# Second MoE's input weights in a fused attention and MoE kernel: a scale for each pair of combined items, made while the pieces are narrowed

## The chip, the core and the metric

The kernel runs on one core of a Trainium2 chip. The metric is the device time of one execution in microseconds (us). Three runs of the kernel before gave 968.54 to 969.66 us.

## What is computed

```python
attn = softmax(rotate(q) @ rotate(k).T / sqrt(64)) @ v      # 4 batches x 8 heads x 576 rows x 64
x  = attn.reshape(2304, 512)
h  = maximum(x @ w1, x @ w2, x @ w3);  x = h @ w_out        # first MoE:  512 -> 768 -> 512
h  = x @ w_in;  g = h * sigmoid(h);  out = g @ w_out        # second MoE: 512 -> 2048 -> 512
```

The weights arrive as 64-bit floats, everything else as 32-bit. The second MoE's `w_in` has 512 x 2048 numbers, its `w_out` 2048 x 512.

## The kernel before

**Attention** runs over 80 tiles of 128 (or 64) query rows. For each tile TensorE (PE) makes the scores (lines 440, 443, 433, 434), VectorE (DVE) takes the row maximum (`nb`, line 453), ScalarE (ACT) the exponential (460) and the normalisation (472). Four DMAs on SyncE's queue move the result into the turned layout (`pt`, 511), DVE turns its 32 x 32 blocks (533), and PE multiplies by `v` (574, 578). The scores have one PSUM tile, so the next tile's scores wait until ACT has read this one's.

**Filler.** Between the tiles PE gets the first MoE's matmuls (line 673), in groups, by a budget per tile; DVE and ACT take the groups' results out of PSUM (690, 692, 698, 699). What is not done when the last tile has its scores runs after attention, and then the second MoE starts (lines 1071, 1103, 1166). All matmuls of both MoEs split their operands into a high and a low half float, each scaled by a power of two.

**The second MoE's weights** are prepared beside attention, one step per tile and two in every fourth tile, from tile 21 on (`wprep3`, the loop at line 1331). `narrow_w2` (820) first handles `w_in` (`WI`), then `w_out` (`WO`), each in 32 pieces of 128 x 256: SyncE loads a piece as 64-bit numbers (858), ACT and DVE narrow it to 32 bits (229; 241, 248, 249), ACT measures its largest square (155), and SyncE writes it to a scratch in memory (833 for `WI`, 838 for `WO`). When all 32 pieces of `WI` are measured, `scale_a` and `scale_b` make one scale for the matrix: three small DVE operations take the root (`root`, 160 to 162), one the row maximum (263), PE transposes it (122), DVE reduces it (124), PE spreads it by a product with ones (130), and four small DVE operations make the powers of two (145 to 148).

From then on `prep_w8` (954, `wprep4`) reads the scratch back in 16 items of 128 x 512 (965), each four blocks. GpSimd (POOL) makes four sums of blocks (971). ACT casts the eight blocks to the high half (`cast_high`, 948) and DVE makes the low half (`cast_low`, 952), in two casts of 128 x 512 each, and SyncE writes each half item to another scratch, `w8scr` (979), from which the second MoE loads them. `WO`'s scratch is read by `prep_w7` (989) after attention.

**What sets the order.** Each engine runs its instructions in the order of its program; a scheduler makes that order from the order of emission and from `issue_after`, which holds an instruction behind another one (`cast_low` and the narrowing on DVE behind the newest row maximum, `cast_high` behind the newest exponential, the scale's PE steps behind the newest scores). Rings of buffers bound how far the steps run apart: 4 pieces (`z_p`), 2 items (`za_p`), 2 sums (`zs_p`), 3 cast halves (`w8o`).

Of the kernel before, what the change touches and what calls it, by code (L numbers as in the profile page):

```python
# [22 lines left out]
def fused_kernel(  # L23
# [796 lines left out]
    def narrow_w2(W, src, nm):  # L820
# [3 lines left out]
        part = {}  # L824
        M = W.m * 512 // 256
        for n in range(M + 5):
            if n >= 5:
                W.measure(n - 5)
# [10 lines left out]
            if 3 <= n <= M + 2:  # L839
                with tc.issue_after(last["max"]):  # L840
                    W.narrow_low(part.get(n - 3))
                    W.narrow_b(n - 3, part.pop(n - 3, None))
            if 2 <= n <= M + 1:
                if wide:
                    W.t[n - 2] = z_p.tile([P, 256], F32, tag="z", name="z")
                with tc.issue_after(exps[-1]):
                    W.narrow_a(n - 2, part.get(n - 2), low=False)
            if n < M:
                i, o = divmod(n * 256, 512)
                if nm == "wi":  # L850
                    q, c = divmod(i, KC)
                    from_ = src[c * P:(c + 1) * P, q * 512 + o:q * 512 + o + 256]
                else:
                    from_ = src[i * P:(i + 1) * P, o:o + 256]
                if wide:
                    part[n] = z64_p.tile([P, 256], w1.dtype, tag="z64", name="z64")
                    with tc.issue_after(last["load"]):
                        nc.sync.dma_start(out=part[n], in_=from_)
                else:
                    W.t[n] = z_p.tile([P, 256], F32, tag="z", name="z")  # L860
                    nc.sync.dma_start(out=W.t[n], in_=from_)
            yield
        t = W.scale_a(n=M)
        yield
        with tc.issue_after(last["score"]):
            W.scale_b("s" + nm, t)
        yield
# [85 lines left out]

    def prep_w8(step):

        sw = half_of(WI, "wi")
        steps = []

        def item(k):
            f, c = divmod(k, 2)  # L960
            z, w = {}, {}

# [483 lines left out]
```

## Time and profile before

| | |
|---|---|
| three runs, us | 968.85, 968.54, 969.66 |
| the profiled execution, us | 970.68 |
| its span, first to last instruction, us | 969.0 |
| busy, share of the span: PE, DVE, ACT, POOL | 93%, 73%, 63%, 46% |
| granted TensorE clock, mean | 0.983 |
| DMA moved | 146.29 MB |

The profiled execution's time is its span and 1.7 us around it. Busy shares are averages over stages with different limits; the stages are told apart by time. A matmul's end is modelled, so PE's busy time says where PE had nothing at all, not that it ran at its best.

### The profile page before, as it was taken

The numbers are of one execution on the slowest core, as the hardware profiler recorded it, in microseconds if no ns is written. First come the engines' busy times: TensorE is split into PE (matmuls) and PEld (weight loads), VectorE is DVE, ScalarE is ACT, GpSimd is POOL, SyncE is SP. The second block draws the span as 40 slices with busy tenths as digits, with TensorE's granted clock in tenths as the row PEclk, the third lists the DMA queues.
The fourth block names the chain that finished last, engine by engine and source line by source line (L and its number), as shares of the span: only waits on it lengthen the run. The fifth ranks groups of instructions, "written<-read, shape, count | busy, mean of one in ns | idle before, by whom it ended". The sixth has DMA issues, their size and how long they took to land.

```text
span 969.0 us, 19018 instructions
## 1 busy us (share of the span) xinstructions
PE 901.6 (93%) x6802; PEld 669.0 (69%) x6802; DVE 709.6 (73%) x1271; ACT 609.4 (63%) x1405; POOL 441.1 (46%) x482
## 2 busy tenths in 40 slices
PE   3887998999999999989998999999998999999997
PEld 1443665666665666656654687788887888888886
DVE  6779888877788676898887677465786766856654
ACT  1987677757788777789877534363654545545442
POOL 6745485870325502321211047264486467464363
PEclk9799998999999999999999999999999999999999
DMA  6953035858888985899999763273543434424101
GB/s 154 285 146 108 14 100 126 186 110 179 200 172 196 221 159 135 218 241 228 263 223 204 183 206 110 63 230 113 157 158 99 136 122 136 127 87 137 61 1 44
DMA packets 178798, 146.29 MB, mean 151 GB/s; under 512 B 50960, under 2 KB 160272, under 8 KB 178704
## 3 DMA queue, kind: packets, MB, share of 16 engines
q1 hardware_dynamic: 177200, 144.36, 58.0%
q8 instruction: 54, 0.88, 0.4%
q10 hardware_dynamic: 1504, 0.72, 0.3%
q14 instruction: 40, 0.33, 0.1%
HBM read 90.51 MB, written 26.21 MB: 120 GB/s over the span
## 4 chain that ended last, share of the span: by engine, by line
PE 54%; DMA 8%; DVE 8%; ACT 5%; POOL 4%; issue 3%; SPq 3%; DVEq 0%; ACTq 0%; POOLq 0%
PE m L673 12%; PE m L1103 7%; DMA pt<-e 5%; PE mb L1103 5%; PE c L1166 4%; PE b L1166 4%; PE a L1166 3%; PE xp L578 3%; PE s L443 3%; PE mg L673 3%; POOL gsum L1050 2%; PE d L1166 2%; SPq L511 2%; DVE pt L533 1%; DVE nb L453 1%
## 5 line engine op out<-in xcount | busy, mean ns | idle before, releaser
L673 PEld LDWEIGHTS <-w 128*128 128x128 f16 x1632 | 159.1, 98 | 61.0 <-issue 17.8
L673 PE MATMUL m<-x,w 128*128 128x256 f16 (+1 forms) x1356 | 186.9, 286 | 10.6 <-DVE t L692 5.4
L1166 PEld LDWEIGHTS <-g 128*128 128x128 f16 x1485 | 145.8, 98 | 17.2
L1103 PEld LDWEIGHTS <-w8s 128*128 128x128 f16 x1344 | 131.2, 98 | 16.3 <-issue 1.0
L453 DVE TENSOR_REDUCE nb<-s 128x2 f32<-128x1152 f32 (+1 forms) x80 | 98.6, 1233 | 40.7 <-PE s L443 34.1
L460 ACT ACTIVATE e<-s,nb 128x576 f32<-128x576 f32 x144 | 105.3, 736 | 29.8 <-DVE nb L453 27.2
L472 ACT ACTIVATE e<-e,rec 128x576 f32<-128x576 f32 x144 | 104.1, 767 | 9.3 <-DVE rec L470 8.9
L366 POOL TENSOR_TENSOR w<-qk,sin_sb 128x512 f32<-128x512 f32 (+2 forms) x40 | 43.4, 1087 | 128.1 <-DMA qk<-in_q_dram 122.5
L443 PE MATMUL s<-T 64*128 64x512 f32 x256 | 80.7, 701 | 0.0
L578 PE MATMUL xp<-pt,vd 128*64 128x256 f32 (+1 forms) x512 | 76.5, 414 | 0.2 <-DVE pt L533 0.2
L533 DVE STREAM_TRANSPOSE pt<-pt 128x1024 f32<-128x1024 f32 (+1 forms) x60 | 67.7, 1129 | 11.9 <-DMA pt<-e 11.6
L971 POOL TENSOR_TENSOR zs<-za 128x128 f32<-128x128 f32 x32 | 17.1, 554 | 119.9 <-DVE w8o L952 46.1
L1117 POOL TENSOR_TENSOR z<-t 128x256 f32<-128x256 f32 x32 | 27.1, 847 | 89.0 <-DVE t L1109 53.9
L1055 DVE SCALAR_TENSOR_TENSOR g<-gsum,sg,g 128x1024 f16<-128x1024 f32 x36 | 49.2, 1372 | 24.5 <-ACT g L1054 24.1
L1054 ACT ACTIVATE g<-gsum,sg 128x1024 f16<-128x1024 f32 x36 | 40.9, 1143 | 37.8 <-POOL gsum L1050 37.8
L673 PE MATMUL m<-h,wo 128*128 128x256 f16 (+1 forms) x448 | 61.7, 286 | 0.0
L673 PEld LDWEIGHTS <-wo 128*128 128x128 f16 x512 | 49.7, 98 | 14.7 <-issue 2.0
L578 PEld LDWEIGHTS xp<-pt,vd 128*64 128x64 f32 x512 | 35.1, 136 | 34.4 <-issue 12.3
L944 POOL TENSOR_TENSOR z<-z 128x256 f32<-128x256 f32 x32 | 30.1, 964 | 42.1 <-DMA z<-zwo 41.6
L1166 PE MATMUL b<-w,g 128*128 128x256 f16 x376 | 48.5, 273 | 0.0
L1166 PE MATMUL c<-w,g 128*128 128x256 f16 x376 | 48.1, 274 | 0.0
L1166 PE MATMUL a<-w,g 128*128 128x256 f16 x376 | 47.9, 273 | 0.0
(266 smaller groups left out, 1998.1 us busy)
## 6 DMA issues: line engine op xcount, KB each, us to landing
w8s<-w8scr SPq DMA_DIRECT2D x64, 448.0 KB, 4.3
pt<-e SPq DMA_DIRECT2D x192, 128.0 KB, 4.1
z<-in_moe_w_in_dram SPq DMA_DIRECT2D x32, 256.0 KB, 3.6
z<-in_moe_w_out_dram SPq DMA_DIRECT2D x32, 256.0 KB, 3.9
w8scr<-w8o SPq DMA_DIRECT2D x32, 256.0 KB, 3.6
w<-in_moe_w_dram SPq DMA_DIRECT2D x6, 768.0 KB, 5.0
wo<-in_moe_w_dram SPq DMA_DIRECT2D x6, 768.0 KB, 5.4
qk<-in_q_dram SPq DMA_DIRECT2D x32, 128.0 KB, 3.6
```

The lines of the kernel that those rows point to most:

```text
L366: tt(out=w4, in0=t4, in1=sin2, op=ALU.mult)
L443: last["s"] = last["score"] = nc.tensor.matmul(s[:, o:o + 512], qs[r], kt[r], start=True, stop=True).ins
L453: x = nc.vector.tensor_reduce(out=nb[:, 0:m], in_=both(s, 0, 960, 576) if m > 1 else s[:, 0:576], op=ALU.max, axis=AX.X, negate=True)
L460: x = nc.scalar.activation(out=e[:, HK[g]], in_=s[:, SK[g]], func=AF.Exp, bias=nb[:, g:g + 1], accum_out=sm[:, g:g + 1])
L472: nc.scalar.activation(out=e[:, HK[g]], in_=e[:, HK[g]], func=AF.Copy, scale=r[:, g:g + 1])
L533: nc.vector.transpose(out=x, in_=x)
L578: nc.tensor.matmul(xp[r, 0:n], v4[:, g, c, :], turned(c, g), start=False, stop=(c == 3))
L673: x = nc.tensor.matmul(ps[:, 0:n], l, r, start=(first and i == 0), stop=(not more and i == len(passes) - 1))
L1054: nc.scalar.activation(out=h, in_=x, func=AF.Copy, scale=sg_t[jb])
L1055: nc.vector.scalar_tensor_tensor(out=l, in0=x, scalar=sg_t[jb], in1=h, op0=ALU.mult, op1=ALU.subtract)
L1103: nc.tensor.matmul(o, l, r, start=(i == 0), stop=(i == len(passes) - 1))
L1166: x = nc.tensor.matmul(ps, l, r, start=first, stop=last_, skip_group_check=True)
```

## The change

`w_in`'s pieces are loaded in another order and cut: two successive pieces now hold the four blocks of one item, and four successive pieces the two items of a pair. A piece is narrowed straight into its half of the item's tile (`za`, now a ring of four, and `z_p` is gone). As soon as the four pieces of pair f are measured, the pair gets a scale of its own (`scale_m`, `scale_a`, `scale_b`, one step each, `wi_scale`), eight in all. Then the sums and casts of its two items follow in the steps of `narrow_w2` itself, one high and one low cast per step. The scratch `zwi`, its 32 writes and its 16 reads are gone, and so is `prep_w8`. `WO` follows `WI` without a pause, and its scratch is written in 16 writes of two pieces. The one scale of the whole matrix is still made, from the maxima that are there, for the second MoE's activations. Since the second MoE's results now differ in scale from pair to pair, `ch` has eight columns, and the Silu of its first block of 256 rows (`s1`) runs on each 256-column half with its own column: 16 instructions of 128 x 256 where 8 of 128 x 512 stood.

```diff
@@ pools, scratch @@
-    z_p = right("z_p", 4)
...
-    zscr = {nm: dram.tile([P, KC * (F2 // 512) * 512], F32, name="z" + nm) for nm in ("wi", "wo")}
+    zscr = {nm: dram.tile([P, KC * (F2 // 512) * 512], F32, name="z" + nm) for nm in ("wo",)}
@@ narrow_w2 @@
-    def narrow_w2(W, src, nm):
...
-                if nm == "wi":
-                    i, o = divmod(n - 5, 2)
-                    q, c = divmod(i, KC)
-                    half, f = divmod(4 * q + 2 * o, HB)
-                    nc.sync.dma_start(
-                        out=zscr[nm].rearrange("p (f c a i n) -> p f c a i n", c=2, a=2, i=2, n=P)[:, f:f + 2, c % 2, c // 2, half],
-                        in_=W.t[n - 5].rearrange("p (f n) -> p f n", n=P),
-                    )
-                else:
-                    nc.sync.dma_start(out=zscr[nm][:, (n - 5) * 256:(n - 4) * 256], in_=W.t[n - 5])
...
+    half_wi = const.tile([P, HB], F32, name="half_wi")
+    inv_wi = const.tile([P, HB], F32, name="inv_wi")
+
+    def wi_scale(f, m):
+        e = rare.tile([P, 1], F32, tag="wie", name="wie")
+        ei, hi, ii = e.bitcast(I32), half_wi.bitcast(I32)[:, f:f + 1], inv_wi.bitcast(I32)[:, f:f + 1]
+        nc.vector.tensor_scalar(out=e, in0=m, scalar1=2.0 ** -45, scalar2=None, op0=ALU.max)
+        nc.vector.tensor_scalar(out=ei, in0=ei, scalar1=EXPMASK, scalar2=None, op0=ALU.bitwise_and)
+        nc.vector.tensor_scalar(out=hi, in0=ei, scalar1=-1, scalar2=266 << 23, op0=ALU.mult, op1=ALU.add)
+        nc.vector.tensor_scalar(out=ii, in0=ei, scalar1=13 << 23, scalar2=None, op0=ALU.subtract)
+
+    def narrow_w2(WI, WO):
+        part, z, zs, w, ma = {}, {}, {}, {}, {}
+        M = WI.m * 512 // 256
+        which = lambda n: (WI, n) if n < M else (WO, n - M)
+
+        def place(n):
+            W, i = which(n)
+            if n % 2 == 0:
+                z[n // 2] = za_p.tile([P, 4, P], F32, tag="za", name="za")
+            W.t[i] = flat(z[n // 2][:, n % 2 * 2:n % 2 * 2 + 2])
...
+                from_ = wi2[(2 * a + c) * P:(2 * a + c + 1) * P, :].rearrange("p (i f n) -> p f i n", i=2, n=P)[:, f]
...
+        def scale_m(f):
+            m = ma[f] = rare.tile([P, 1], F32, tag="wim", name="wim")
+            nc.vector.tensor_reduce(out=m, in_=WI.maxima(4 * f, 4), op=ALU.max, axis=AX.X)
+
+        def scale_a(f):
+            with tc.issue_after(last["score"]):
+                ma[f] = all_max_a(ma[f])
+
+        def scale_b(f):
+            with tc.issue_after(last["score"]):
+                m = all_max_b(ma.pop(f))
+            wi_scale(f, m)
...
+        for n in range(2 * M + 6):
+            for f in range(HB):
+                if 7 <= n - 4 * f <= 9:
+                    (scale_m, scale_a, scale_b)[n - 4 * f - 7](f)
...
+                for at_, g, q, h in ((10, low, k, 0), (11, low, k + 1, 0), (12, low, k, 1), (13, low, k + 1, 1)):
+                    if s == at_:
+                        g(q, h)
...
+                for at_, g, q, h in ((9, high, k, 0), (10, high, k + 1, 0), (11, high, k, 1), (12, high, k + 1, 1)):
...
+                if s in (8, 9):
+                    sums(k + s - 8)
...
+            if n >= M + 4 and n % 2 and n <= 2 * M + 3:
+                i = n - 4 - M
+                nc.sync.dma_start(out=zscr["wo"][:, (i - 1) * 256:(i + 1) * 256], in_=flat(z.pop((n - 4) // 2)))
@@ y_scales @@
-        ch = small.tile([P, 1], F32, tag="ch", name="ch")
-        nc.vector.tensor_scalar(out=ch, in0=co, scalar1=2.0 * w, scalar2=None, op0=ALU.mult)
+        ch = small.tile([P, HB], F32, tag="ch", name="ch")
+        nc.vector.tensor_scalar(out=ch, in0=inv_wi, scalar1=i, scalar2=2.0 * w, op0=ALU.mult, op1=ALU.mult)
@@ prep_w8, removed whole @@
-    def prep_w8(step):
...
-                nc.sync.dma_start(out=flat(z[0]), in_=zscr["wi"][:, (2 * f + c) * 512:(2 * f + c + 1) * 512])
...
-            for d, fn in ((0, load), (2, sums), (2.1, lambda: high(0)), (2.9, lambda: low(0)), (3, lambda: high(4)), (3.9, lambda: low(4))):
@@ s1 @@
-                nc.scalar.activation(
-                    out=g[:, 2 * half:2 * half + 2].rearrange("p t (i n) -> p i t n", i=2),
-                    in_=ps.rearrange("p (i t n) -> p i t n", i=2, t=2), func=AF.Silu, scale=ch,
-                )
+                for e in range(2):
+                    nc.scalar.activation(
+                        out=g[:, 2 * half:2 * half + 2, e * P:e * P + P],
+                        in_=ps[:, e * 256:e * 256 + 256].rearrange("p (t n) -> p t n", t=2), func=AF.Silu, scale=ch[:, 2 * u + e:2 * u + e + 1],
+                    )
@@ main loop @@
-    wprep3, wprep4 = narrow_all(), None
+    wprep3 = narrow_w2(WI, WO)
...
+            za_p.bufs = 4
             for _ in range(1 + (j % 4 == 0) if j > 20 else 0):
                 next(wprep3, None)
-            if hasattr(WI, "s"):
-                wprep4 = wprep4 or prep_w8(1.7)
-                next(wprep4, None)
```

**The order, first place.** DVE, from the row maximum of the 38th tile to that of the 39th, before (line numbers of each kernel's own file; `z` are pieces, `t`, `h` the first MoE's results):

```order
L453 TENSOR_REDUCE nb_3027<-s_3023 128x2
L533 STREAM_TRANSPOSE pt_2846<-pt_2846 128x1024
L241 TENSOR_SCALAR z_2_2872<-z_2_2872 128x256
L248 TENSOR_SCALAR z_2971<-z_2971 128x256
L692 SCALAR_TENSOR_TENSOR t_3156<-m_3143,t_3141 128x256
L249 SCALAR_TENSOR_TENSOR z_2971<-z_2_2872,z_2971 128x256
L692 SCALAR_TENSOR_TENSOR t_3171<-m_3158,t_3156 128x256
L470 RECIPROCAL rec_3102<-rec_3102 128x2
L699 TENSOR_TENSOR h_6_3173<-t_3171,h_6_3173 128x256
L453 TENSOR_REDUCE nb_3095<-s_3091 128x2
```

The same place now (`w8o` is a cast, `amax` a step of a pair's scale):

```order
L449 TENSOR_REDUCE nb_3142<-s_3138 128x2
L529 STREAM_TRANSPOSE pt_2939<-pt_2939 128x1024
L1020 SCALAR_TENSOR_TENSOR w8o_3077<-zs_2891,half_wi_141,w8o_3077 128x512
L240 TENSOR_SCALAR z_2_2968<-z_2_2968 128x256
L247 TENSOR_SCALAR za_3084<-za_3084 128x256
L123 TENSOR_REDUCE amax_3070<-tr_3068 1x1
L688 SCALAR_TENSOR_TENSOR t_3288<-m_3275,t_3273 128x256
L248 SCALAR_TENSOR_TENSOR za_3084<-z_2_2968,za_3084 128x256
L466 RECIPROCAL rec_3231<-rec_3231 128x2
L688 SCALAR_TENSOR_TENSOR t_3303<-m_3290,t_3288 128x256
L449 TENSOR_REDUCE nb_3224<-s_3220 128x2
```

One cast and one scale step have come in; one tile earlier 23 instructions now stand between two row maxima, three casts among them, where 10 stood. Counted over the order, the 32 low casts stand between the 29th and the 55th row maximum now, and behind the 55th before; between these two, 32 pieces are narrowed where 25 were.

**Second place.** DVE between the 64th and the 65th row maximum, before:

```order
L453 TENSOR_REDUCE nb_5182<-s_5178 128x2
L533 STREAM_TRANSPOSE pt_4985<-pt_4985 128x1024
L241 TENSOR_SCALAR z_3_4936<-z_3_4936 128x256
L248 TENSOR_SCALAR z_5130<-z_5130 128x256
L952 SCALAR_TENSOR_TENSOR w8o_5141<-za_4940,wihalf_4184,w8o_5141 128x512
L249 SCALAR_TENSOR_TENSOR z_5130<-z_3_4936,z_5130 128x256
L241 TENSOR_SCALAR z_0_5012<-z_0_5012 128x256
L248 TENSOR_SCALAR z_5220<-z_5220 128x256
L249 SCALAR_TENSOR_TENSOR z_5220<-z_0_5012,z_5220 128x256
L692 SCALAR_TENSOR_TENSOR t_5418<-m_5405,t_5343 128x256
L470 RECIPROCAL rec_5266<-rec_5266 128x2
L453 TENSOR_REDUCE nb_5259<-s_5255 128x2
```

and now:

```order
L449 TENSOR_REDUCE nb_5434<-s_5430 128x2
L529 STREAM_TRANSPOSE pt_5254<-pt_5254 128x1024
L240 TENSOR_SCALAR z_2_5218<-z_2_5218 128x256
L247 TENSOR_SCALAR za_5391<-za_5391 128x256
L578 SCALAR_TENSOR_TENSOR x_3917<-xp_5441,vs_3555,x_3917 128x320
L688 SCALAR_TENSOR_TENSOR t_5638<-m_5625,t_5577 128x256
L248 SCALAR_TENSOR_TENSOR za_5391<-z_2_5218,za_5391 128x256
L240 TENSOR_SCALAR z_3_5280<-z_3_5280 128x256
L247 TENSOR_SCALAR za_5391<-za_5391 128x256
L466 RECIPROCAL rec_5510<-rec_5510 128x2
L688 SCALAR_TENSOR_TENSOR t_5653<-m_5640,t_5638 128x256
L248 SCALAR_TENSOR_TENSOR za_5391<-z_3_5280,za_5391 128x256
```

The cast is gone from here, as from all tiles behind the 55th row maximum.

**Third place.** SyncE's queue around the 39th tile, before (`zwi` is the scratch of `w_in`, `pt` attention's moves):

```order
L858 DMA z_2_3404<-in_moe_w_in_dram 128x256
L833 DMA zwi_137<-z_3244 128x2x128
L308 DMA qk_3941<-in_k_dram 64x2x64
L511 DMA pt_3377<-e_3302 32x8x128 x4
L315 DMA vd_0_129<-in_v_dram 128x2x256
L320 DMA vd_0_129<-in_v_dram 64x64
L858 DMA z_3_3505<-in_moe_w_in_dram 128x256
L833 DMA zwi_137<-z_3342 128x2x128
```

and now:

```order
L304 DMA qk_3943<-in_k_dram 64x2x64
L860 DMA z_3_3375<-in_moe_w_in_dram 128x2x128
L507 DMA pt_3236<-e_3226 32x8x128 x4
L316 DMA vd_0_126<-in_v_dram 64x64
L876 DMA w8scr_133<-w8o_3190 128x2x512
L876 DMA w8scr_133<-w8o_3252 128x2x512
L316 DMA vd_0_126<-in_v_dram 64x64
L876 DMA w8scr_133<-w8o_3370 128x2x512
L507 DMA pt_3236<-e_3313 32x4x128
```

The scratch's writes are gone, and the writes of cast halves (`w8scr`) stand among attention's moves instead. Over the whole program SyncE has 395 rows where it had 456, DVE 1,330 where it had 1,262. The first MoE's matmuls move too: 424,448 of their columns stood behind the last tile's scores, and 412,288 do now; of the 12,160 that moved forward, 8,000 stand ahead of the 55th tile's scores and 4,160 behind them.

## Rows read from the trace of the kernel before

**Rows 1.** stretches: span, busy us (instructions) of PE, PEld, DVE, ACT, POOL; clock, DMA share, GB/s

```profile
218.00:378.00 160.00, 155.71 (x1052) 100.56 (x1052) 121.58 (x239) 121.00 (x344) 41.25 (x44) 1.00 0.84 179
378.00:537.00 159.00, 147.53 (x981) 93.30 (x978) 134.34 (x265) 131.97 (x364) 38.27 (x65) 1.00 0.92 226
537.00:624.00 87.00, 84.56 (x670) 64.37 (x669) 53.79 (x101) 37.01 (x70) 30.12 (x32) 1.00 0.47 132
...
760.00:969.00 209.00, 203.51 (x1863) 182.00 (x1860) 133.58 (x223) 96.70 (x147) 106.65 (x119) 0.99 0.31 94
```

**Rows 2.** who waited for whom on DVE, 218 to 378: us in total, times, longest

```profile
DVE nb L453 <- PE s L443: 15.1, 14, 2.9
...
DVE nb L453 <- PE s L434: 4.8, 4, 2.3
```

**Rows 3.** three shorter stretches, same columns as Rows 1

```profile
340.00:377.00 37.00, 37.00 (x244) 23.75 (x241) 24.69 (x52) 25.92 (x68) 0.00 (x0) 1.00 0.73 130
400.00:420.00 20.00, 18.99 (x133) 12.42 (x132) 19.55 (x37) 16.55 (x46) 3.75 (x8) 1.00 0.90 238
400.00:500.00 100.00, 94.08 (x650) 61.75 (x649) 88.60 (x176) 86.53 (x242) 18.03 (x36) 1.00 0.95 241
```

**Rows 4.** casts (tile w8o) alone, 378 to 537: DVE, ACT; clock, DMA share, GB/s

```profile
378.00:537.00 159.00, 23.46 (x29) 21.01 (x30) 1.00 0.92 226
```

**Rows 5.** two stretches, narrowed pieces (tile z) alone: DVE, ACT, POOL

```profile
218.00:378.00 160.00, 29.68 (x76) 23.56 (x77) 0.00 (x0) 1.00 0.84 179
378.00:537.00 159.00, 32.77 (x93) 28.01 (x91) 0.00 (x0) 1.00 0.92 226
```

**Rows 6.** DVE in order of time, 553 to 554.4: start, us, instruction

```profile
553.89 0.14 DVE L147 TENSOR_SCALAR swos<-swoe 128x1 int32<-128x1 int32 x1
553.95 0.14 DVE L148 TENSOR_SCALAR swoi<-swoe 128x1 int32<-128x1 int32 x1
554.07 0.15 DVE L939 TENSOR_SCALAR wohalf<-swos 128x1 f32<-128x1 f32 x1
```

**Rows 7.** DVE groups, 218 to 378: busy us, mean ns | idle before

```profile
L241 DVE TENSOR_SCALAR z<-z 128x256 uint16<-128x256 uint16 x25 | 14.1, 564 | 0.0
...
L249 DVE SCALAR_TENSOR_TENSOR z<-z,z 128x256 int32<-128x256 int32 x26 | 12.4, 477 | 0.2
```

**Rows 8.** DVE groups, 232 to 262

```profile
L241 DVE TENSOR_SCALAR z<-z 128x256 uint16<-128x256 uint16 x6 | 2.6, 427 | 0.0
L249 DVE SCALAR_TENSOR_TENSOR z<-z,z 128x256 int32<-128x256 int32 x6 | 2.5, 419 | 0.1
```

**Rows 9.** two more stretches, same columns as Rows 1

```profile
232.00:262.00 30.00, 30.00 (x206) 19.44 (x205) 20.87 (x43) 22.79 (x68) 3.24 (x3) 1.00 0.85 192
624.00:650.00 26.00, 26.00 (x241) 23.30 (x239) 14.79 (x14) 16.64 (x23) 16.58 (x16) 1.00 0.70 220
```

**Rows 10.** groups of the whole span: POOL's sums, ACT's first Silus, a copy

```profile
L971 POOL TENSOR_TENSOR zs<-za 128x128 f32<-128x128 f32 x32 | 17.1, 554 | 119.9 <-DVE w8o L952 46.1 <-DMA za<-zwi 27.4 <-DVE pt L533 13.1
...
L1110 ACT ACTIVATE t<-m 128x256 f32<-128x256 f32 x32 | 11.9, 373 | 9.6 <-PE m L1103 9.4
...
L971 POOL TENSOR_TENSOR zs<-za,zs 128x128 f32<-128x128 f32 x16 | 7.6, 477 | 1.1
...
L1072 ACT ACTIVATE ga<-m,ch 128x512 f32<-128x512 f32 x4 | 2.7, 677 | 0.0
```

**Rows 11.** the scale's product with ones (line 130), 150 to 560: time, and who waited

```profile
L130 PE MATMUL tr<-amax,ones x8: 245/256/266, 298.8 to 552.9; 1*128 1x1 f32 x8
...
  DVE swoe L145: 2.1, 1
  DVE swo1e L145: 0.9, 1
```

**Rows 12.** the chain of waits, one piece of it: start, us, what

```profile
654.17 2.62 PE m L1103 x24
```

**Rows 13.** who waited on DVE, 378 to 537

```profile
DVE pt L533 <- DMA pt<-e: 6.6, 3, 3.5
```

More of the change, by code (lines that the diff above doesn't have):

```diff
@@ L260, in row_max @@
         def row_max(self, lo=0, n=None, ma=None):
-            ma = ma or self.maxima(lo, n or self.m)
+            ma = self.maxima(lo, n or self.m) if ma is None else ma
             m1 = rare.tile([P, 1], F32, tag="wm1", name="wm1")
@@ L818, in fused_kernel @@
     NQ = F2 // 512
[L820 to L839 removed]
+    HB = NF2 // 2
@@ L840, in narrow_w2 @@
                 with tc.issue_after(last["max"]):
                     W.narrow_low(part.get(n - 3))
-                    W.narrow_b(n - 3, part.pop(n - 3, None))
-            if 2 <= n <= M + 1:
+                    W.narrow_b(i, part.pop(n - 3, None))
+            for f in range(HB):
+                k, s = 2 * f, n - 4 * f
+                for at_, g, q, h in ((9, high, k, 0), (10, high, k + 1, 0), (11, high, k, 1), (12, high, k + 1, 1)):
+                    if s == at_:
+                        g(q, h)
+                if s in (8, 9):
+                    sums(k + s - 8)
@@ L844, in narrow_w2 @@
+            if 2 <= n <= 2 * M + 1:
+                W, i = which(n - 2)
                 if wide:
-                    W.t[n - 2] = z_p.tile([P, 256], F32, tag="z", name="z")
+                    place(n - 2)
                 with tc.issue_after(exps[-1]):
[L847 to L861, printed above, removed]
@@ L862, in narrow_w2 @@
-            yield
[L863 to L867, printed above, removed]
+                    W.narrow_a(i, part.get(n - 2), low=False)
+            if 3 <= n <= 2 * M + 2:
+                W, i = which(n - 3)
+                W.measure(i)
+            if n >= M + 4 and n % 2 and n <= 2 * M + 3:
+                i = n - 4 - M
+                nc.sync.dma_start(out=zscr["wo"][:, (i - 1) * 256:(i + 1) * 256], in_=flat(z.pop((n - 4) // 2)))
@@ L952, in cast_low @@
             nc.vector.scalar_tensor_tensor(out=l, in0=x, scalar=s, in1=h, op0=ALU.mult, op1=ALU.subtract)
-    def prep_w8(step):
[L956 to L961, printed above, removed]
-            def load():
-                z[0] = za_p.tile([P, 4, P], F32, tag="za", name="za")
-                nc.sync.dma_start(out=flat(z[0]), in_=zscr["wi"][:, (2 * f + c) * 512:(2 * f + c + 1) * 512])
-            def sums():
-                z[4] = zs_p.tile([P, 4, P], F32, tag="zs", name="zs")
-                block = lambda i: z[i // 4 * 4][:, i % 4]
-                for o, x, y, op in SUMS:
-                    nc.gpsimd.tensor_tensor(out=block(o), in0=block(x), in1=block(y), op=op)
-            def high(a):
-                w[a] = w8o_p[0].tile([P, 2, 4, P], F16, tag="w8o", name="w8o")
-                cast_high(flat(w[a][:, 0]), flat(z[a]), sw, exps[-1])
-            def low(a):
-                cast_low(flat(w[a][:, 1]), flat(w[a][:, 0]), flat(z[a]), sw, last["max"])
-                nc.sync.dma_start(out=w8scr[:, f, c, :, a:a + 4], in_=w[a])
-            t = k * step
-            for d, fn in ((0, load), (2, sums), (2.1, lambda: high(0)), (2.9, lambda: low(0)), (3, lambda: high(4)), (3.9, lambda: low(4))):
-                steps.append((t + d, fn))
-        for k in range(2 * HB):
-            item(k)
-        yield from timed(steps)
     def prep_w7(stage, w7_p, w7, step):
@@ L1120, in s1_pair @@
                 x = g[:, :, e * P:e * P + P]
-                nc.scalar.activation(out=x, in_=x, func=AF.Silu, scale=ch)
+                nc.scalar.activation(out=x, in_=x, func=AF.Silu, scale=ch[:, p:p + 1])
             if e:
@@ L1355, in fused_kernel @@
     for _ in wprep3:
-        pass
-    for _ in wprep4:
         pass
```

53 lines of the change are left out of this document (46 added, 7 removed).

## The prediction

> **What bounds the kernel now.** I read the stretches first [rows 1]. From 624 us on there is nothing to win here: from 760 to 969 TensorE (PE) is busy for 203.5 of 209 us, and the change touches little of it. The work that moves lies in two stretches. Stretch A, 218 to 378 us, holds the tiles from the 29th to the 55th row maximum, stretch B, 378 to 537 us, the rest of attention. The clock is 1.00 in both. PE is busy for 155.7 of A's 160 us and 147.5 of B's 159, so it has nothing at all to do for 4.3 us in A and 11.5 us in B. The side engines are loaded unevenly: VectorE (DVE) is busy for 121.6 us in A (76%) and 134.3 us in B (84%), ScalarE (ACT) for 121.0 and 132.0, DMA 0.84 and 0.92. Then I ask what DVE's idle time in A is. Of 38.4 us it waits 19.9 us for the scores of the next tile [rows 2]: DVE waits for PE there, not PE for DVE. In B DVE waits for attention's moves as well. Last I look for stretches that show a light and a full DVE [rows 3]. From 340 to 377 us, between `w_in`'s narrowing and the casts, DVE is busy for 24.7 of 37 us (67%) and PE has no idle time. From 400 to 500 us DVE is busy for 88.6% and PE idles 5.9 us; the densest 20 us have DVE at 97.8%, with PE idle for 1.0 us. So the kernel is bound by PE where the side work is light, and loses about 6% of PE's time where DVE nears nine tenths.
>
> **The change, part by part.** By the order the change moves all casts from B to A, adds eight scale chains to A, narrows 7 more pieces in A, and takes SyncE's scratch traffic out. The tiles themselves stay.
>
> *DVE in A.* In B the 29 low casts cost DVE 23.46 us, 0.81 us each [rows 4]; 32 are 25.9 us. The narrowing keeps DVE busy for 32.77 us in B on 93 instructions, three to a piece: 1.06 us a piece [rows 5]. The 7 further pieces are 7.4 us. A scale is nine small DVE instructions: three for the root, two reductions, four for the powers. Such ones last 0.14 to 0.15 us, but the next begins after 0.06 or 0.12 us where it needs nothing of it [rows 6]; I take 0.12 us, since most of a chain's steps depend on each other, and 72 are 8.6 us (bounds 4.3 and 10.8). Sum: 121.6 + 25.9 + 7.4 + 8.6 = 163.5 us of work in a stretch of 160 us. **DVE cannot do it in A's time**, so A becomes longer. At the share of the densest 20 us (97.8%) A takes 167.2 us, at the share of the long stretch (88.6%) 184.5 us. I take 92%, a little nearer the long row, because A is long and the order is bunched (23 instructions between two row maxima where 10 stood): 177.7 us, **17.7 us more**. ACT gets 32 x 0.70 = 22.4 us of casts [rows 4] and 7 x 0.92 = 6.5 us of pieces [rows 5], which makes 149.9 us: it stays under the new length and costs nothing of its own. If DVE had the room, ACT at 94% of 160 us would be late next.
>
> *POOL's sums* move along. Over all of A, with POOL busy for 41.25 us [rows 1], line 241 took 564 ns and line 249 477 ns [rows 7]; from 232 to 262 us 427 and 419 ns [rows 8], with POOL busy for 3.24 of 30 us [rows 9]. That is 25 x 0.137 + 26 x 0.058 = 4.9 us that DVE lost beside POOL. The sums are 17.1 us and twice 7.6 us, one row each for the two like groups [rows 10]: 32.3 us more on POOL in A, and at the same rate 3.8 us more on DVE. The Trainium skill, "Perfetto Trace Analysis", section on optimizing Scalar and DVE operations, says that GpSimd and DVE share an SBUF read port, and that a two-port DVE operation holds it alone; that speaks against putting the sums beside a full DVE. The trace agrees with the direction, by 564 against 427 ns. I leave the 3.8 us out of the sum, since B's price of a piece already holds sums beside it, and give it to a rival.
>
> *PE in A.* The scale chains add 8 transposes and 8 products with ones, 0.26 us each if a transpose lasts like a product [rows 11], 4.2 us, and 8,000 columns of the first MoE come forward, at 109 ns for 256 columns (24 matmuls in 2.62 us [rows 12]) 3.4 us. Both find room in A's 177.7 us, in which PE had 155.7 us of busy time. Cover gone, that is if A did not stretch, they would cost 7.6 us.
>
> *SyncE in A.* The scratch's writes go, and 32 writes of cast halves come. Each waits for a low cast on DVE, and the next `pt` moves and loads stand behind it. In B, where they stand today, DVE waited 6.6 us for moves [rows 13]; A shows no such wait. I take 0, inside the stretch already, with 6.6 us as the upper end. The four-deep ring of items lets ACT's narrowing wait for the low cast that reads the tile last; that, too, is within A's stretch or ACT's free tenth.
>
> *B.* It loses 29 casts and 6 pieces: 134.3 - 23.5 - 6.4 = 104.4 us, 66% of 159 us, the share of the light stretch in which PE had no idle time [rows 3]. DMA falls as well, by the item reads and the cast halves. So I give B back all of PE's idle time, 11.5 us, less the 4,160 columns that come to it (1.8 us): **9.7 us less**. Half of the idle time less those columns, 3.9 us, is the other end.
>
> *Behind attention* 12,160 columns less stand before the second MoE, 47.5 x 0.109 = **5.2 us less**, on a PE that is busy for 84.6 of 87 us there [rows 1]. The scale of `w_out` and its last pieces are done before the last tiles; at most the other 2.4 us of PE's idle time go too.
>
> *Nothing:* the 16 Silus of half size, 373 ns for a like 256-column copy against 677 ns for 512 [rows 10], add 0.6 us to ACT, busy for 16.6 of 26 us there, beside a PE without a gap [rows 9]; uncovered, they would cost those 0.6 us. The wider `ch` is five small instructions as before.
>
> *Sum:* +17.7 - 9.7 - 5.2 = **+2.8 us**. The profiled execution took 970.68 us, 1.8 us over the median of the three runs; 970.68 + 2.8 = 973.5 us would be its like, and against the median, 968.85 us, I forecast **971.7 us**. About 1.9 us (0.2%) is what a measurement of this kernel can tell from no change.
>
> **Rivals.**
>
> 1. *DVE fills its waits* (faster). Over half of DVE's idle time in A is waiting for PE's scores [rows 2], and work put there delays nobody. At 97.8% A costs only 7.2 us: 968.85 + 7.2 - 9.7 - 5.2 = 961.2 us. It decides from a share of 94.5% on, where A costs 13.0 us. For it: the densest 20 us. Against: no long stretch over 88.6%, and the bunching.
> 2. *The two balance* (no change): A's share between 92.5% and 94.5%, A 17 to 13 us longer, 967 to 970.8 us.
> 3. *The scale chains stop PE* (slower). PE runs in order, and each scale gives it two steps that wait for DVE, while DVE's first step of the powers waits for PE's product. Of the earlier chains two cost DVE 2.1 and 0.9 us, and the others nothing shown [rows 11]. Eight at 1.0 to 2.1 us on top of the stretch are 8 to 17 us: 980 to 989 us. For it: a full DVE answers late. Against: steps are a tile apart in the order.
> 4. *POOL beside DVE.* By the rates above DVE's 163.5 us become 167.3 us, at 92% 4.1 us more: 975.8 us. It is the port rule of the page named above, made with this kernel's rows.
>
> That the change does not do what it says is excluded by the order: the scratch's transfers are gone and the casts stand where described.
>
> **Chances.** My forecast, A at a share of 88.6% to 92.5%, 0.33; rival 1, 0.28; rival 2, 0.20; rival 3, 0.11; rival 4, 0.08. So faster 0.28, within 0.2% 0.20, slower 0.52. The outer ends are A full at 100% with all of the tail's idle gone (3.5 - 9.7 - 7.6: 955 us) and A at 88.6% with SyncE's and the chains' worst and half of B's return (24.5 + 6.6 + 17 - 3.9 - 5.2: 1008 us); neither needs to be held. The range runs from rival 1 to the lower part of rival 3: **961 to 985 us**. It holds both signs; the forecast's own is 970.8 to 978.5 us.
>
> **What would show it.** Right: a stretch from the 29th to the 55th tile of 175 to 181 us with DVE over 90% busy and PE idle for over 10 us; PE's idle time behind it down to a few us, DVE at two thirds; the first MoE's rest some 5 us shorter. Rival 1 shows as DVE near 97% in a stretch of under 173 us, rival 3 as waits of PE's lines 121 and 129 (as numbered now) or of DVE's line 825 on them, rival 4 as narrowing over 0.6 us an instruction. I am wrong if B does not get its idle time back, if SyncE's queue makes DVE wait for moves in A, or if the second MoE itself changes its time.

## The result, and the profile after

The changed kernel took 981.29 us, the median of four runs (980.89 to 981.66); the kernel before, beside it, 968.69 us. The ratio is 1.0133 (95% interval 1.0118 to 1.0148): 12.6 us slower. The forecast was 971.7 us, with a range of 961 to 985 us. The profiled executions differ by 10.2 us (980.89 against 970.68), and the row maxima of the 29th, 55th and 80th tile say where:

| us | before | after | difference | forecast |
|---|---|---|---|---|
| start to 29th | 218.3 | 216.3 | -2.0 | 0 |
| A, 29th to 55th | 159.2 | 182.5 | +23.3 | +17.7 |
| B, 55th to 80th | 159.8 | 155.8 | -4.0 | -9.7 |
| behind the 80th | 431.7 | 424.6 | -7.1 | -5.2 |

A and B of the kernel before between the same row maxima, with the columns of [rows 1]:

```profile
218.30:377.50 159.20, 154.91 (x1046) 100.21 (x1048) 120.92 (x238) 120.70 (x344) 41.25 (x44) 1.00 0.85 179
377.50:537.30 159.80, 148.33 (x985) 93.83 (x984) 135.00 (x266) 132.25 (x365) 38.27 (x65) 1.00 0.92 225
```

The changed kernel's stretches: A, B, and the rest of the first MoE behind them.

```profile
216.30:398.80 182.50, 170.07 (x1095) 106.70 (x1095) 162.64 (x355) 144.15 (x396) 71.88 (x92) 0.97 0.84 194
398.80:554.60 155.80, 152.56 (x1005) 96.45 (x1007) 110.64 (x228) 113.15 (x323) 9.32 (x9) 1.00 0.74 152
...
554.60:633.60 79.00, 77.54 (x617) 59.51 (x618) 51.42 (x84) 32.45 (x59) 30.71 (x32) 1.00 0.38 116
```

DVE did 162.6 us of work in A, and the sum had 163.5. But A is not 92% full of it, only 89%, and the mean clock fell to 0.97. TensorE is idle for 12.4 us (4.3 before) and busy for 15.2 us more. Twenty of A's 23 us stand in nine tiles, from the 37th to the 46th row maximum: 55.4 us before, 75.7 now. Of the signs that the prediction gave, A's 175 to 181 us and DVE's 90% were missed by a little, and PE's idle time of over 10 us came. Six pieces of 4 us from there:

```profile
272.00:276.00 4.00, 2.95 (x25) 2.15 (x23) 4.00 (x11) 3.15 (x9) 3.27 (x6) 1.00 0.79 238
276.00:280.00 4.00, 2.65 (x17) 1.93 (x17) 4.00 (x7) 3.58 (x13) 0.96 (x3) 0.84 0.56 163
280.00:284.00 4.00, 4.00 (x21) 2.09 (x22) 2.92 (x6) 2.88 (x7) 1.54 (x3) 0.73 0.81 226
300.00:304.00 4.00, 0.58 (x2) 0.39 (x3) 4.00 (x7) 3.92 (x16) 0.68 (x2) 0.83 0.47 134
304.00:308.00 4.00, 4.00 (x14) 1.81 (x15) 3.04 (x8) 2.42 (x8) 1.48 (x3) 0.50 0.81 225
308.00:312.00 4.00, 4.00 (x30) 3.05 (x29) 4.00 (x8) 2.04 (x6) 3.58 (x3) 0.82 0.94 191
```

PE idles 2.4 us between 272 and 280 and 3.4 us between 300 and 304, and the granted clock falls behind both, the second time to 0.50, its 1.2 GHz level; over these rows what is missing to 1.00, times 4 us, adds up to 5.1 us. That is an estimate from above of what the clock cost, since PE had nothing to do in part of that time. What PE does then takes longer: the large score matmuls, whose number is the same, took 22.6 us in A before and 26.7 us now (mean 641 and 691 ns; one row of each kernel, over A).

```profile
L443 PE MATMUL s<-T 64*128 64x512 f32 x80 | 22.6, 641 | 0.0
```

```profile
L439 PE MATMUL s<-T 64*128 64x512 f32 x80 | 26.7, 691 | 0.0
```

PE's idle time in A stands ahead of instructions that wait for another engine, most of it for ACT; the two largest rows are (total, times, longest):

```profile
PE s L436 <- ACT e L456: 4.0, 2, 2.2
PE tr L518 <- ACT kd L407: 3.2, 2, 1.9
```

What stands behind these waits from 297 to 306 us is in the timeline (start, us, engine, instruction; in brackets the idle time ahead of it and what ended it):

```profile
297.57 0.71 ACT L1016 ACTIVATE w8o<-zs,half_wi 128x512 f16<-128x512 f32 x1
...
299.19 1.00 DVE L248 SCALAR_TENSOR_TENSOR za<-z,za 128x256 int32<-128x256 int32 x2
...
299.63 0.42 ACT L154 ACTIVATE junk<-za 128x256 bf16<-128x256 f32 x1 [1.35 <-DVE za L248]
...
300.11 1.34 DVE L449 TENSOR_REDUCE nb<-s 128x2 f32<-128x1152 f32 x1
...
300.71 0.45 ACT L407 ACTIVATE kd<-tr 64x64 f32<-64x64 f32 x2
...
301.21 0.33 PE L518 MATMUL tr<-ident,e 128*128 128x128 f32 x1 [1.89 <-ACT kd L407]
...
302.14 0.73 ACT L456 ACTIVATE e<-s,nb 128x576 f32<-128x576 f32 x1
...
302.86 0.74 ACT L456 ACTIVATE e<-s,nb 128x576 f32<-128x576 f32 x1
...
303.75 0.79 PE L436 MATMUL s<-kd,T 128*128 128x128 f32 x2 [2.21 <-ACT e L456]
...
304.47 2.08 PE L439 MATMUL s<-T 64*128 64x512 f32 x4
```

DVE narrows first and takes the row maximum only from 300.1 on. ACT's queue has a cast, then the measuring of a piece, which waits 1.35 us for DVE's narrowing; behind that stand the copies of the next batch's turned q and k (`kd`), whose PSUM tile PE's next transpose needs, and the exponential, for which PE's next scores wait. At this place three queues in order hold one another, and the work that holds them is the preparation's; other places were not followed this closely.

### The profile page after: what moved, and what is told of

Its sections match the earlier page's. It is cut to its first block, busy times and chain, and to the rows that moved or that the text cites. A ratio compares the mean times of both kernels' runs of the same rounds, so it can differ in the third digit from the quotient of the medians.

```text
span 979.2 us, 19042 instructions
## 1 busy us (share of the span) xinstructions
PE 913.7 (93%) x6826; PEld 673.1 (69%) x6826; DVE 723.4 (74%) x1339; ACT 611.2 (62%) x1413; POOL 447.6 (46%) x482
## 4 chain that ended last, share of the span: by engine, by line
PE 48%; DVE 5%; DMA 5%; ACT 3%; POOL 3%; issue 2%; SPq 1%; DVEq 0%; ACTq 0%; POOLq 0%
PE m L669 9%; PE m L1137 7%; PE mb L1137 5%; PE c L1200 4%; PE b L1200 4%; PE a L1200 3%; PE mg L669 3%; PE xp L574 3%; POOL gsum L1083 2%; PE s L439 2%; PE d L1200 2%; DMA pt<-e 1%; PE mb L1104 1%; PE m L1104 1%; PE m L1200 1%
## 5 line engine op out<-in xcount | busy, mean ns | idle before, releaser
L456 ACT ACTIVATE e<-s,nb 128x576 f32<-128x576 f32 x144 | 105.3, 737 | 29.4 <-DVE nb L449 26.7
L439 PE MATMUL s<-T 64*128 64x512 f32 x256 | 84.3, 713 | 0.0
L574 PE MATMUL xp<-pt,vd 128*64 128x256 f32 (+1 forms) x512 | 79.6, 415 | 0.4 <-DVE pt L529 0.4
L363 POOL TENSOR_TENSOR qk<-qk,cos_sb 128x512 f32<-128x512 f32 (+2 forms) x44 | 48.9, 1114 | 2.5
```

Source lines behind the costliest of these rows:

```text
L363: tt(out=t4, in0=t4, in1=cos2, op=ALU.mult)
L439: last["s"] = last["score"] = nc.tensor.matmul(s[:, o:o + 512], qs[r], kt[r], start=True, stop=True).ins
L456: x = nc.scalar.activation(out=e[:, HK[g]], in_=s[:, SK[g]], func=AF.Exp, bias=nb[:, g:g + 1], accum_out=sm[:, g:g + 1])
L574: nc.tensor.matmul(xp[r, 0:n], v4[:, g, c, :], turned(c, g), start=False, stop=(c == 3))
```

## The experiments

Theory at first: A is as long as DVE's work in it. Rivals: the scale chains stop PE; POOL beside DVE; later the bunching of the order, and ACT. Each run was timed beside the kernel before (median 968.3 us for e1 to e4, 968.2 for e7 to e9, 967.9 for e10 to e12, 969.1 for e13 and e14). All measured values at once, sorted by A; those with a star do all the work.

| run | A us | DVE, ACT busy in A | clock in A | B us | median us | ratio to before |
|---|---|---|---|---|---|---|
| e14, before with one edit* | 161.4 | 123.0, 120.4 | 1.00 | 159.2 | 973.8 | 1.0061 (1.0038 to 1.0084) |
| e7, narrowing only | 162.5 | 130.0, 124.4 | 1.00 | 155.8 | 965.1 | 0.9960 (0.9941 to 0.9979) |
| e9, no casts | 169.6 | 140.5, 124.0 | 0.99 | 156.7 | 968.9 | 1.0005 (0.9990 to 1.0019) |
| e3, even pacing* | 172.1 | 150.2, 135.6 | 0.97 | 156.7 | 974.5 | 1.0058 (1.0041 to 1.0076) |
| e8, no step while turning* | 173.9 | 148.1, 132.9 | 1.00 | 158.2 | 978.8 | 1.0120 (1.0086 to 1.0153) |
| e12, e11's edit and even pacing* | 174.4 | 149.9, 132.3 | 0.99 | 167.4 | 987.0 | 1.0192 (1.0175 to 1.0208) |
| e11, measuring held behind* | 175.5 | 157.8, 141.0 | 0.97 | 153.8 | 972.8 | 1.0073 (1.0038 to 1.0108) |
| e2, no sums | 176.4 | 157.6, 142.7 | 0.97 | 156.6 | 978.4 | 1.0108 (1.0079 to 1.0137) |
| e4, no low casts | 177.1 | 140.1, 142.6 | 0.97 | 154.9 | 974.5 | 1.0056 (1.0033 to 1.0079) |
| e10, no high casts | 178.3 | 160.1, 123.8 | 0.97 | 156.0 | 975.1 | 1.0066 (1.0044 to 1.0088) |
| e1, one chain | 179.3 | 158.6, 142.2 | 0.97 | 156.1 | 976.5 | 1.0084 (1.0055 to 1.0113) |
| e13, e11's edit, other pacing* | 181.3 | 162.9, 141.6 | 0.99 | 161.9 | 984.8 | 1.0165 (1.0131 to 1.0200) |
| the change* | 182.5 | 162.6, 144.2 | 0.97 | 155.8 | 981.3 | 1.0133 (1.0118 to 1.0148) |

A's time is of the profiled execution, which lies up to 3.8 us off the median of its kernel (most in one chain). A does not hold the same work of PE in all runs either. Counted in the traces, the first MoE has 185,088 columns in A before, 192,448 in the changed kernel, and from 182,848 (e11) to 198,208 (e13) in the others; e1, e2, e3, e7 and e8 have within 640 of the kernel before. At the prediction's 109 ns for 256 columns, about 3 us of what these five save in A against the change, and 4.1 us in e11, is work that PE does elsewhere. So the kernel's time is read first, and A beside it.

**One chain for all pairs.** The first pair's scale is written to all eight columns.

```diff
-                if 7 <= n - 4 * f <= 9:
+                if f == 0 and 7 <= n <= 9:
```

> The scale chain of the first pair alone is made and written to all eight columns; the other seven (63 small DVE instructions, 14 PE steps, in the changed kernel's stretch A together some 10 us of DVE's busy time) are left out, so the scales of seven pairs are not those of their own maxima. Theory (A is as long as DVE's work in it, at about 89% share): 10 us of DVE work less shorten A by 8 to 11 us, 981.3 becomes 970 to 974 us. Rival, the chains stop PE by their two steps in PE's order: more than their busy time comes back, A falls under 169 us and the kernel under 967 us. Rival, POOL or the bunched order alone make A long: under 4 us come back, 977 us or more.

976.5 us: 4.8 us back, half of what the theory wanted, 0.5 us outside the third reading (977 us or more) and nothing like the second's. In the changed kernel PE's steps of the chains had 0.5 us of idle time ahead of them in all of A. There the chains do not stop PE; in the run without high casts, further down, they do, for 3.5 us in two waits.

**No sums.**

```diff
-            for o, x, y, op in SUMS:
-                nc.gpsimd.tensor_tensor(out=block(o), in0=block(x), in1=block(y), op=op)
```

> POOL's 64 sums of blocks in the preparation of w_in are left out (the casts of the second halves read the blocks themselves), DVE's and ACT's work stays. Theory (DVE's amount of work): the narrowing falls from 492 to about 430 ns an instruction and the casts a little, 4 to 7 us of DVE work less, A 4 to 8 us shorter, 973 to 977 us. Rival, POOL beside DVE is the main cause of A's growth (with the stalls that follow from it): A back to about 168 us, 967 us or less. Rival, no contention to speak of: within 1.5 us of 981.3 us.

978.4 us; 2.9 us back, in none of the three ranges, and with an interval that overlaps the change's own. The narrowing's first step hardly got faster (its row: 530 ns with the sums, 525 without), the last one did (535 to 469).

**Even pacing.**

```diff
-            for _ in range(1 + (j % 4 == 0) if j > 20 else 0):
+            for _ in range(1 + (j % 4 == 0 and j > 50) if j > 20 else 0):
```

> Same work, other pacing: one step of the weights' preparation per tile, and two in every fourth tile only behind tile 50, so six or seven of the steps in A move to B. Theory (A is DVE bound and B has room, DVE at 71%): the narrowing, casts and scales of six steps, some 14 us of DVE work, leave A, which becomes 12 to 16 us shorter; B gets 2 to 6 us longer; 969 to 974 us. Rival, only the sum of the work over A and B counts, wherever it stands: no change, 979 to 983 us. Rival, the stalls come with each cast or chain, not with the load: A and B exchange about equal amounts, 978 us or more.

974.5 us, A 10.4 us shorter, B 0.9 us longer. The theory was nearly met here, each of its three ranges missed by a little.

**No low casts.**

```diff
-            cast_low(flat(t[:, 1]), flat(t[:, 0]), flat((z, zs)[a][k]), half_wi[:, f:f + 1], last["max"])
-            nc.sync.dma_start(out=w8scr[:, f, c, :, 4 * a:4 * a + 4], in_=t)
+            for x in range(2):
+                nc.sync.dma_start(out=w8scr[:, f, c, x, 4 * a:4 * a + 4], in_=t[:, 0])
```

> The 32 low casts on DVE are left out (the high half is written to both places of the scratch), and nothing else: 24.4 us of DVE work less in A. Theory: A shortens by 20 to 24 us to 159 to 163 us, with DVE near 138 us of it, and PE's idle time there falls under 5 us; 957 to 962 us. Rival, the scale chains or POOL's sums make A long: A stays above 172 us, 970 us or more.

974.5 us, and A at 177.1 us with DVE at 79% in it:

```profile
217.60:394.70 177.10, 168.01 (x1091) 106.93 (x1090) 140.07 (x323) 142.61 (x396) 64.39 (x92) 0.97 0.91 200
```

**Here the theory fell**: 22.6 us less DVE work shortened A by 5.4 us, at the same lower clock. The rival named (A over 172 us) has the number, but the first two runs, which take out its causes one at a time, gave back only 4.8 and 2.9 us. The edit is not clean, though: it makes 64 writes of cast halves out of 32, and PE's longest gap in A stands behind such a write:

```profile
274.95 0.72 ACT L1016 ACTIVATE w8o<-zs,half_wi 128x512 f16<-128x512 f32 x1 [3.25 <-DMA w8scr<-w8o]
...
276.25 0.45 ACT L407 ACTIVATE kd<-tr 64x64 f32<-64x64 f32 x2
...
276.75 0.33 PE L518 MATMUL tr<-ident,e 128*128 128x128 f32 x1 [2.66 <-ACT kd L407]
```

In the changed kernel the high casts waited 1.9 us for a write in all of A. The price of the low casts without this doubling is the step from no casts to no high casts, below. So ACT came under suspicion, whose casts the sum had at nothing, and the parts were taken out from the other end.

**Narrowing only**: sums, casts and seven chains out.

```diff
-            cast_high(flat(t[:, 0]), flat((z, zs)[a][k]), half_wi[:, k // 2:k // 2 + 1], exps[-1])
...
+            nc.sync.dma_start(out=w8scr[:, f, c, :, 4 * a:4 * a + 4], in_=w[0])
```

> All that the change added to stretch A beside the narrowing is left out: the sums, both casts and seven of the eight chains (the cast halves written out are a constant). What stays of the change: the pieces' new order and cut, seven more of them in A, the 32 writes on SyncE, 8,000 more columns on PE. Theory (A is PE's work plus PE's stalls, and the stalls and the lower clock behind them come from the preparation's amount beside attention's own work): A comes back to 160 to 165 us at a clock of 0.99 to 1.00, the kernel to 960 to 965 us. Rival (the order of the pieces, their narrower loads, the ring of four or the writes on SyncE make the stalls): A stays over 170 us at 0.97, 968 us or more.

**No casts**: the same with sums and all chains kept.

> The 32 high casts on ACT and the 32 low casts on DVE are left out (a constant is written out in their place); sums and all eight chains stay. Theory (casts of both engines in their two queues make the stalls, as leaving out the low ones alone gave back 7 us): A falls to 163 to 170 us, the kernel to 961 to 969 us. Rival (chains and sums, with the denser narrowing, are enough for the stalls): A stays at 173 us or more, 972 us or more.

965.1 and 968.9 us. The stretches A and B of the first, then of the second:

```profile
220.00:382.50 162.50, 156.56 (x1048) 100.39 (x1050) 130.02 (x261) 124.36 (x365) 38.96 (x36) 1.00 0.91 169
382.50:538.30 155.80, 155.74 (x1034) 99.15 (x1036) 109.65 (x228) 113.17 (x323) 9.32 (x9) 1.00 0.73 154
```

```profile
218.30:387.90 169.60, 161.26 (x1074) 103.88 (x1073) 140.52 (x323) 124.00 (x364) 62.55 (x91) 0.99 0.84 164
387.90:544.60 156.70, 154.90 (x1024) 98.22 (x1024) 109.53 (x229) 113.47 (x323) 9.48 (x9) 1.00 0.75 153
```

Both theories were met, but for 0.1 us of the first kernel's time. With the narrowing alone A is within 3.3 us of what it was before, at full clock: order and cut of the pieces, and the seven more, are not the cause. The ring and the writes are not the cause by themselves; that a cast holds a buffer of the ring, or a write waits for a cast, does not come up in these two runs. (The columns that the change moved into A stayed in B here.) Chains and sums together add 3.8 us to the kernel, all casts, with the waits that hang on them, another 12.4 us. Without casts, DVE is as busy as without the low ones (140.5 and 140.1 us); between these two runs stand ACT's 32 high casts, 18.6 us of its time, and 5.6 us of the kernel's, the doubled writes of the one included. What the casts cost where they stood before, in B, no run measures.

**No step while q and k are turned.**

```diff
+            for _ in range((j not in (37, 40, 43, 54, 57, 60, 63)) + (j in (46, 48, 50, 52) or j > 60 and j % 2) if j > 20 else 0):
```

> Same work, third pacing: no step of the preparation in the seven tiles in which the next batch's q and k are turned (37, 40, 43, 54, 57, 60 and 63), one step in the others, two at tiles 46, 48, 50, 52 and in every odd tile from 61 on. Theory (the stalls come where attention's own bunch and the preparation's meet): A at 163 to 168 us with a clock of 0.99, B 156 to 160 us, 964 to 970 us. Rival (only the amount within A counts, as in the even pacing): 973 to 976 us, like that one.

978.8 us, neither's number. The clock stays at 1.00 in A, and yet PE idles 11.8 of 173.9 us:

```profile
218.30:392.20 173.90, 162.09 (x1072) 102.61 (x1073) 148.11 (x314) 132.85 (x365) 63.70 (x84) 1.00 0.80 176
```

**No high casts.** The low ones subtract a constant.

```diff
-            cast_high(flat(t[:, 0]), flat((z, zs)[a][k]), half_wi[:, k // 2:k // 2 + 1], exps[-1])
+            cast_low(two(t[:, 1]), ident.bitcast(F16).unsqueeze(1).to_broadcast([P, 2, 256]), two((z, zs)[a][k]), half_wi[:, f:f + 1], last["max"])
```

> The 32 high casts on ACT alone are left out; the low casts on DVE stay (they subtract a constant, and their result is written out twice). 19.9 us of ACT's work less in A, DVE's work as in the changed kernel. Theory (ACT's casts have a price of their own, as the step from no casts, 968.9 us, to high casts alone, 974.5 us, says): A 173 to 178 us, the kernel 974 to 977.5 us. Rival (A follows DVE's work alone, with ACT hidden under it, as the prediction's sum had it): within 2 us of 981.3 us.

975.1 us: as expected (A 0.3 us over its range), 6.2 us back with 2.6 us less of DVE's work:

```profile
219.10:397.40 178.30, 166.43 (x1087) 105.58 (x1087) 160.06 (x354) 123.84 (x359) 67.61 (x92) 0.97 0.84 197
```

Against the run without casts it has the 32 low casts alone: 19.5 us more of DVE's work, for 8.7 us of A and 6.2 us of the kernel, with 32 writes in both (which wait for the casts here).

**Measuring held behind the exponential.**

```diff
+            if 4 <= n <= 2 * M + 3:
+                W, i = which(n - 4)
+                with tc.issue_after(exps[-1]):
+                    W.measure(i)
```

> Same work; each piece's measuring on ACT is emitted one step later and held behind the newest exponential, so that ACT's queue no longer stands behind DVE's last step of the narrowing (it waited 9.3 us for it in A of the changed kernel, 6.7 us before). Theory (A grows by what one engine's queue makes the others wait in order, so a wait taken out of ACT's queue comes back in part): the wait of the measuring falls under 3 us in A, A 175 to 179 us, the kernel 974 to 978 us. Rival (A is DVE's amount of work; ACT's waits cost nothing): within 2 us of 981.3 us. Rival (ACT then waits for the row maxima in their place): the wait is gone and another of like size stands on ACT, 980 us or more.

972.8 us, 1.2 us under the theory's range, and 0.73% slower than before. By its median it is the fastest order of the change; by the ratios it is not told apart from the even pacing. The measuring's wait fell from 9.3 to 1.2 us in A, but part of it stands elsewhere on ACT (6.1 us for `rec` and 4.3 us for `nb` in the changed kernel):

```profile
ACT e L456 <- DVE nb L449: 8.6, 11, 1.5
ACT e L468 <- DVE rec L466: 8.3, 9, 1.6
```

PE gained nothing by it in A. The stretches A and B:

```profile
218.10:393.60 175.50, 162.78 (x1066) 103.61 (x1066) 157.78 (x355) 140.97 (x389) 67.75 (x92) 0.97 0.83 198
393.60:547.40 153.80, 153.73 (x1029) 98.21 (x1030) 111.05 (x228) 114.82 (x329) 9.50 (x9) 1.00 0.76 159
```

PE idles 12.7 us in A, where it was 12.4 in the changed kernel, at the same clock. A has 9,600 columns less, 4.1 us, and 8,000 of them fill B, where PE's idle time falls from 3.2 to 0.1 us. So this run does not show that ACT's wait was the price; A's gain is in good part that the first MoE's columns went to B.

**The same with even pacing, and with a fourth pacing.**

> The even pacing (one step per tile up to tile 50) and the measuring behind the exponential together, all work kept. Theory (the two are independent): the even pacing's 974.5 us less 3 to 7 us, 967 to 971.5 us, so level with the kernel before. Rival (the measuring's wait costs nothing): 973 to 976 us.

> All work kept; the measuring held behind the exponential, and a fourth pacing: two steps at tiles 24, 28 and 32, one at each of 33 to 45, two at 46, 47, 49, 50, 52 and 53, so that the last casts are done before the next batch's q and k are turned from tile 54 on. Theory (queues stand still where attention's turning and the preparation meet, so both meetings must be thinned): the tiles 37 to 46 in 63 to 66 us where they took 70.5 us, A 168 to 172 us, B 154 to 157 us, the kernel 966 to 970 us. Rival (any further change of the order moves the stalls elsewhere and gains nothing): 972 us or more.

987.0 and 984.8 us: both theories missed by 14 us or more; the second's rival (972 us or more) came. Two edits that gave 6.8 and 8.5 us singly lose 5.7 us together. In the first, B is 11.6 us longer than in the changed kernel: 2.7 us by 6,400 more columns, the rest mostly by stalls and the clock, most of these where the last casts meet the next turning (420 to 440 us of the even one, at a clock of 0.83):

```profile
420.00:440.00 20.00, 16.20 (x90) 10.11 (x88) 15.20 (x38) 14.00 (x40) 0.00 (x0) 0.83 0.85 216
```

**The kernel before with the measuring held behind.**

```diff
+                with tc.issue_after(exps[-1]):
+                    W.measure(n - 5)
```

> The kernel before with one edit: the measuring on ACT held behind the newest exponential. Theory (the measuring's wait is a price that the change's load in A brought out: ACT waited 6.7 us for it in A before and PE lost little by it): within 2 us of the kernel before. Rival (the wait costs any kernel of this shape alike, so that taking it out is no part of the change's story): 5 us or more faster.

973.8 us, 4.7 us slower, where one reading wanted no change and the other a gain. ACT's wait for the measured pieces (15.7 us over A and B) went, and its wait for `rec` grew from 3.8 to 20.1 us (two rows of the kernel before, then one of this run):

```profile
ACT junk L155 <- DVE z L249: 15.7, 17, 3.6
...
ACT e L472 <- DVE rec L470: 3.8, 6, 0.9
```

```profile
ACT e L472 <- DVE rec L470: 20.1, 21, 3.4
```

## Why the prediction was right or wrong

**Right by its range and its side**, but the number owes some of that to luck: 981.3 us lies above the forecast's own 970.8 to 978.5 us, in the part of the range that came from rival 3, whose mechanism did not come. By the profiled executions A grew 5.6 us more than forecast and B gave back 5.7 us less, while the start and the tail gave 3.9 us that were not forecast. What was right besides: the amounts of work (DVE 162.6 us against 163.5 in A, 110.6 against 104.4 in B), most of B's idle time returned (3.2 us left of 11.5), DVE without a wait for attention's moves in A (0.0 us ahead of line 529), the first MoE's rest shorter, and a second MoE that lasts as long as before (345.6 and 345.1 us from its first matmul to the end). Of DVE's terms in A the casts came to 26.5 us (25.9 in the sum). The rows of the scales' small steps add up to 16.0 us and overlap with others; with seven chains of eight left out DVE had 4.0 us less to do in A, where 8.6 us stood for eight. Single ones are slow beside a busy POOL: of the seven of line 160 three took 1.15 to 1.25 us, POOL working through each, and four, with POOL idle, 0.16 to 0.17 us (the rows of A, changed kernel):

```profile
L1020 DVE SCALAR_TENSOR_TENSOR w8o<-za,half_wi,w8o 128x512 f16<-128x512 f32 x16 | 14.8, 942 | 0.8 <-ACT w8o L1016 0.8
...
L1020 DVE SCALAR_TENSOR_TENSOR w8o<-zs,half_wi,w8o 128x512 f16<-128x512 f32 x16 | 11.7, 729 | 0.0
...
L160 DVE TENSOR_SCALAR wi2m<-wi2m 128x4 int32<-128x4 int32 x7 | 4.3, 610 | 0.1
```

**The step that failed is the price of A**: at 92%, 177.7 us. It takes A to be DVE's work over a share. A's length does not go by that: 140 us of DVE work made 169.6 us without casts and 177.1 us with ACT's casts and doubled writes, and 160 us made 178.3. DVE's share of A ran from 79% to 90% in the runs of the change. By PE it nearly closes: 8,000 columns and 16 chain steps, 7.6 us by the prediction's prices; the lower clock, at most 5.1 us; idle time, 8.1 us more. These are 20.8 of 23.3 us; the other 2.5 us are open. The same sum, with the columns and chains counted in each trace, comes within 3.5 us of A in every run. The prediction had put the 7.6 us into A's growth as hidden work ("Both find room"), and had no term for the clock. PE's idle time is waiting for ACT and DVE in the middle of its queue: the work that came forward did not fill it, it grew beside it.

**ACT "costs nothing of its own"** was wrong as well, as far as these runs tell. Taking out the high casts gave 6.2 us, the low ones 6.8 us (6.2 us by the step without doubled writes), both 12.4 us: about 0.2 us of the kernel for each cast on either engine, with the waits that hang on it, where the sum had 28 us for the low ones' work (25.9 us at 92%) and nothing for the high ones. That the total came out near is an overpriced term beside missing ones.

**B**: +4.2 us of PE's busy time came instead of 1.8, and 3.2 us of idle time stayed, so 4.0 us and not 9.7 were returned. 2.4 us of it are not explained by columns. Line by line they stand in attention's products with `v` (line 578 before, 23.7 us in 158 matmuls; line 574 now, 27.4 us in 162); why is open.

**Behind attention** the first MoE's rest fell from 86.6 to 79.0 us, by 7.6 us. PE's busy time fell by 6.7 us, of which the columns are 5.2; of its 2.4 us of idle time, the prediction's upper end on top, 1.0 us went.

**Rivals.** DVE filling its waits came by half (it waits 10.2 us for scores, 19.9 before [rows 2]), and nothing was saved by it. The chains as stops of PE: 0.5 us in the changed kernel, so not the cause, though in the run without high casts PE waited 3.5 us for the pairs' maxima, with which a chain begins. POOL beside DVE: of the rates in [rows 7, 8] little belongs to the sums, for without any sums the narrowing took 542 and 539 ns:

```profile
L240 DVE TENSOR_SCALAR z<-z 128x256 uint16<-128x256 uint16 x32 | 17.4, 542 | 0.6 <-ACT za L228 0.5
L248 DVE SCALAR_TENSOR_TENSOR za<-z,za 128x256 int32<-128x256 int32 x32 | 17.3, 539 | 0.2
```

That is the kernel with narrowing only; POOL's turning of q and k runs there as everywhere. The direction of the port rule of the Trainium skill ("Perfetto Trace Analysis", section on optimizing Scalar and DVE operations) shows in line 160's steps; the narrowing's last step took 535 ns with the sums, and without them 469 ns in one run and 539 in the other. The sums' share of this change, 2.9 us, is not clear of none.

**What stays open.** Reordering alone, with all the work done, spans 972.8 to 987.0 us, and one edit of the order cost the kernel before 4.7 us. By the kernel's time none of the six reorderings came out in the range of its theory. So the single prices of 3 to 7 us above may hold some of that; the steps of 12.4 us (casts) and 16.2 us (all but the narrowing) are beyond what any reorder moved against the change itself (8.5 us at most), though a second pacing on top of e11 moved 14.2 us; they rest on two runs that agree in their stretches (A at a clock of 1.00 and 0.99, with 5.9 and 8.3 us of PE's idle time) as much as on the times. How the stalls come about was read at one place each of two traces, and the four orders that were meant to thin them (e8, e11 to e13) left PE 10 us or more of idle time in A. In the places shown the clock falls behind PE's gaps; that was not tried by itself. No version with all the work was faster than the kernel before.

## What to carry to other kernels

This case suggests: when work moves into a stretch that one in-order engine fills, price the stretch by that engine: its own new work in full, plus the waits that the other queues give it, plus the clock behind long waits. A side engine's busy share, even a well counted one, does not give the length. And before reading a difference of half a per cent as the price of a part, see what a mere reorder of the same work does.

## What the runs showed of the hardware

The clock was lost in a stretch that PE filled to 93%. PE idled 2.4 us of 8 and 3.4 us of 4, and behind each the granted clock fell; the missing 5.1 us make some 10 us at the 1.2 GHz level, and are two thirds of what all the moved columns and chain steps take (7.6 us). In the run without steps in the turning tiles PE idled nearly as long in A (11.8 us, against 12.4) at a clock of 1.00, so the sum of the idle time alone does not tell whether the clock falls.

DVE's steps on 128 x 4 numbers (line 160) took seven times as long, 1.15 to 1.25 us for 0.16 to 0.17, where POOL worked through them; but not always: in the run without casts one took 0.17 us beside a busy POOL.
